# Q's weight quarters issued in another order, Q's last rows on GpSimd's queue, two transposes moved between half passes, K1's copy on ScalarE

## The chip, the core and the metric

The kernel runs on one NeuronCore of a Trainium2 chip. The metric is the device time of one execution in microseconds (us); lower is better. All moments below are counted from the start of the profiled span.

## The reference

Input x has 2048 tokens of 576 numbers (bf16). It is normalized without scale or shift, and two blocks read the result xn; their outputs and x itself are added:

```python
xn = _layernorm(x, axis=-1)
return x + _A_ref(xn, A_wqkv, A_wo) + _B_ref(xn, B_w_gate, B_w_up, B_w_down)
```

Block A is linear attention with 32 heads of 18: q, k, v = xn @ wqkv; phi(t) = (t + 1 if t > 0 else exp(t)) + 1e-6 is applied to q and k; kv and z are sums over all tokens, the head output is (phi(q) kv) / (phi(q) z + 1e-6), and wo follows. Block B is (gelu(xn @ w_gate) * (xn @ w_up)) @ w_down with 4608 hidden columns. The two blocks share nothing but xn.

## The kernel before

**Tiling.** The 2048 tokens are 16 tiles of 128 tokens ("tile n"; 0 to 15). A contraction over the 576 columns takes four chunks of 128 rows (`kt` 0 to 3) and one of 64 (`kt` 4, "the ends"). `_Unit` (L239 to L281) computes a product as two half passes: TensorE is used as two row groups of 64 (LO and HI), which write two banks of PSUM (the matmul accumulators) at the same time. In the first half pass, `rows`, LO writes the left half of the output and HI the right one; in the second, `p2`, they swap. Between the two, the row groups have to take turns on a bank: `swap` puts a semaphore wait on GpSimd's queue (POOL) that TensorE's second half pass waits for. It is called the unit's *turn*.

**The head.** What the change touches is the first 17 us or so. There the kernel loads x tile by tile, computes statistics and norms, brings xn into the transposed layout `xnT` (or, for tiles 0 and 1, the centred copy `xcT`), and starts the products K0, K1, Q0, Q1 and so on (`_Token`: K or Q of one tile) as soon as inputs are there. The gate-and-up units g0, g1 and so on (`_Raw`) come next, and from there the rest of the kernel follows.

For tile n below 4 the chain is: load of x; `stats` in two halves and `aggr` (VectorE, DVE); `rstd` (ScalarE, ACT); `norm` (DVE); `transposes` (TensorE, L359 to L362; called t0 to t3 below) into two PSUM banks; `tp_copy` (L364 to L367), which copies one bank to `xnT` on ScalarE and the other on VectorE. Tile 1 has its mean and square sum from ScalarE. Tiles 0 and 1 are transposed before their rstd is known; rstd is multiplied in when their product is copied out by `raw` (K0 and Q0 on ScalarE, K1 and Q1 on VectorE).

**Loads.** `x` of tiles 0 to 3 are single loads of 144 KB. K's columns of wqkv (rows 0 to 511) are one load of 576 KB. Q's are four quarters of 144 KB: rows LO or HI of each chunk, left or right half of the columns. Named here by rows and half, Q's first half pass reads LO-0 and HI-1, its second LO-1 and HI-0. The rows 512 to 575 of K and of Q, the ends, are two small loads each (`load_w_ends`), read at the end of a second half pass. `wr` holds the ends of gate and up (`load_ends`). Loads are issued on SP's queue unless another is named, and in the order of the program. The framework hands eight completion semaphores in turn to the loads issued by SP and by ScalarE, and the ninth load waits until the first holder has landed. So, before, LO-1 waits for the load of K's columns, and HI-0 for x of tile 1.

**Order of the work.** The head's steps are listed as `step(...)` with an engine, an assumed duration, a rank and what they come after. `in_order` (L77 to L94) plays them through once with those assumed times and writes the instructions in the order found, so a changed assumption (`X_AT`, `DMA_FREE`, a `ready`) can reorder an engine's queue, which the hardware then executes strictly in that order. TensorE's order alone is fixed by hand in `line`: a name is the first half pass of a unit, "t2" the transposes of tile 2. In the kernel before, a second half pass follows as soon as two units are open; "." forces one.

Before, the queues are:

- TensorE: t0, t1, K0 first, K1 first, K0 second, Q0 first, K1 second, t2, Q1 first, Q0 second, K2 first, Q1 second, Q2 first, K2 second, t3, Q2 second, K3 first, Q3 first, K3 second, g0 first, and so on.
- VectorE around tiles 2 and 3: stats and aggr 2, norms 1 and 2, raw K1, its half of the copy of t2, stats and aggr 3, norm 3, raw Q1, its half of the copy of t3, then phi of K2 and Q2.
- POOL: K's ends (2 loads), the copies `twin` that pad x, tile 1's mean, the ends of gate and up (2 loads), twin 2, turns K0, K1 and Q0, the load of x for tiles 4 and 5, turn Q1, twin 3 (which waits for x of tile 3), turn K2 and so on.
- SP: x0, K's columns, x2, LO-0, HI-1, x3, LO-1, HI-0, the DMA transpose of tile 0 (`xnU` 0), wg and wu of block 0, wg of block 1, the DMA transpose of tile 1, x of tiles 6 and 7, and so on. x1 and Q's ends are issued by ScalarE.

Of the kernel before, what the change touches and what calls it, by code (L numbers as in the profile page):

```python
# [25 lines left out]
TPC = SC // P  # L26
HALF = D // 2
# [12 lines left out]
RAW = 14  # L40
# [7 lines left out]
CENTRED = (0, 1)  # L48
# [40 lines left out]
def kernel(  # L89
# [29 lines left out]

    SYNC = mybir.DependencyInfo(mybir.DependencyClass.Sync, mybir.DependencyReason.DATA)  # L120
    LO, HI = slice(0, HP), slice(HP, P)
    banks, head_banks = _Ring([6, 7, 2, 3, 4, 5, 0, 1]), _Ring([4, 5, 6, 7, 2, 3, 4, 5, 6, 7, 2, 3, 4, 5, 0, 1])

    def two_banks(ring=banks):
        return [ring.next(), ring.next()]
# [43 lines left out]
    def load_w_quarters(which, halves):  # L169

        for rows, half in zip((LO, HI), halves):
            c = which * D + half * HALF
            view = A_wqkv[0:4 * P, c:c + HALF].rearrange("(kt p) c -> p kt c", p=P)
            nc.sync.dma_start(wqkv_sb[rows, 0:4, c:c + HALF], view[rows])  # L174
# [9 lines left out]

    gu_blocks, wr_pairs = {}, {}

    def load_ends(i, on=nc.sync):
        c = slice(GUB * P * (i % NB), GUB * P * (i % NB + 2))
        wr = wr_pairs[i // 2] = wr_bufs.next()
        on.dma_start(wr[LO, :], B_w_gate[512:576, c])  # L190
        on.dma_start(wr[HI, :], B_w_up[512:576, c])

    def load_gu(i, part):

# [187 lines left out]

    for n in range(4, NS, 2):
        on, sp, at = ("POOL", 0.75, 9.2) if n == 4 else ("SP", 0.58, 6.0)
        load(("x", n), sp, 295, 9.0 if n == 4 else 7.0 + 2.5 * (n - 10), [("turn", "Q0")] * (n == 4), lambda n=n: load_x(n, 2, nc.gpsimd if n == 4 else nc.sync), ready=at, on=on)
    step("ends", "POOL", 1.4, 3.0, [("mean", 1)], lambda: load_ends(0, nc.gpsimd))

    for n in range(NS):
        first = 1.5 * n if n < 4 else 9.0 + 3.0 * (n - 4)
        both = n // 2 * 2  # L390
        after_x = [("x", both)] if n >= 4 else []
        x_at = X_AT[n] if n < 4 else 12.6 if n < 8 else 2.1 * both + 3.0
        if n < 4:
            step(("twin", n), "POOL", 0.2, first, [], lambda n=n: x_twin(n, 1), ready=10.1 if n == 3 else x_at)
        elif n == both:
            step(("twin", n), "POOL", 0.25, first, after_x, lambda n=n: x_twin(n, 2), ready=max(2.6 * n + 3.0, 14.6))
        twin = ("twin", n if n < 4 else both)
        if n != 1:
            for h in range(2):
                step(("stats", n, h), "DVE", 0.42, first, after_x + [("raw", "K1")] * (n == 3) + [("phi", "Q2")] * (n == 4) + [("phi", "K5")] * (n in (12, 13)), lambda n=n, h=h: ln_half(n, h), ready=x_at)  # L400
            step(("aggr", n), "DVE", 0.2, first, [("stats", n, 0), ("stats", n, 1)], lambda n=n: ln_aggr(n), tail=0.05)
        if n in CENTRED:
            if n:
                step(("sum", n), "ACT", 0.78, first - 3.0, [], lambda n=n: act_sum(n), ready=x_at)
                step(("mean", n), "POOL", 0.54, first - 3.0, [("sum", n)], lambda n=n: act_mean(n), tail=-0.27)
                step(("aggr", n), "ACT", 0.95, first + 2.0, [("mean", n), ("xnT", 1, 0)], lambda n=n: act_square(n))
            mean = ("mean", n) if n else ("aggr", n)
            step(("centre", n), "DVE", 0.45, first - 0.5, [mean, twin], lambda n=n: centre(n), tail=0.05)
        if n not in (1, 2) and n < 6:
            step(("rstd", n), "ACT", 0.5, first - 2.0 * (n == 3), [("aggr", n)], lambda n=n: ln_rstd(n, 1))  # L410
        elif n == both:
            m = min(n, 1) if n < 6 else n
            step(("rstd", n), "ACT", 0.46, first, [("aggr", m), ("aggr", m + 1)], lambda m=m: ln_rstd(m, 2))
            if n == 2:
                steps[("rstd", 1)] = _Step("none", 0.0, first, [("rstd", 2)], lambda: None, 0.0, 0.0)
        ready = [("rstd", n if n < 6 else both), twin]
        if NORM[n] == "A":
            step(("bias", n), "POOL", 0.27, first, ready[:1], lambda n=n: ln_bias(n))
            ready.append(("bias", n))
        on, took = ("ACT", 0.92) if NORM[n] == "A" else ("DVE", 0.45)  # L420
        if n < HEAD:
            late = n in CENTRED
            step(("norm", n), on, took, 2.5 if late else first, ready + [("tp", n)] * late, lambda n=n: ln_norm(n), tail=0.05)
            step(("tp", n), "PE", 0.2, 0, [("centre" if late else "norm", n)], lambda n=n: transposes(n), tail=0.15)
            for i, copied in enumerate((0.44, 0.30)):
                step(("xnT", n, i), "DVE" if i else "ACT", copied, first - 1.0, [("tp", n)], lambda n=n, i=i: tp_copy(n, i), tail=0.02)
            steps[("xnT", n)] = _Step("none", 0.0, first, [("xnT", n, 0), ("xnT", n, 1)], lambda: None, 0.0, 0.0)
            if late:
                load(("xnU", n), 1.25, 80, first + 2, [("norm", n)], lambda n=n: dma_transposes(n))
        else:  # L430
            step(("norm", n), on, took, first, ready, lambda n=n: ln_norm(n), tail=0.05)
            load(("xnT", n), 1.25, 80, first + 2, [("norm", n)], lambda n=n: dma_transposes(n))

    class _Token:
# [14 lines left out]

        def raw(self):  # L450
            dst = (pk if self.kind == "K" else pq)[:, self.n, :].rearrange("p (h c) -> p h c", h=2)
            if self.n == 0:
                nc.scalar.activation(out=dst, in_=self.acc, func=ACT.Identity, scale=rstd[:, 0:1])
            elif self.n == 1:
                nc.vector.tensor_scalar(out=dst, in0=self.acc, scalar1=rstd[:, self.n:self.n + 1], scalar2=None, op0=ALU.mult)
            else:
                nc.scalar.copy(out=dst, in_=self.acc)
            self.acc = dst
# [28 lines left out]
                out=hT[:, self.f:self.f + NF + 1:NF, :], in_=ps_all[:, self.two[0]:self.two[0] + 2, :],  # L487
            )

    line = ["t0", "t1", "K0", "K1", "Q0", "t2", "Q1", "K2", "Q2", "t3", ".", "K3", "Q3"] + [f"g{i}" for i in range(LEAD)]  # L490
    for i in range(12):
        line += [f"K{i + 4}"] + ([f"g{i + LEAD}"] if i + LEAD < RAW else [])

    owner, pending = {}, []

# [23 lines left out]
    def p2_step(u):  # L519
        n = int(u.name[1:])  # L520
        pe(("p2", u.name), u.t2, [("turn", u.name)], u.unit_p2)
        if u.name[0] in "KQ":
            later = u.name in RAW_T
            if later:
                step(("raw", u.name), *(("DVE", 0.76) if n == 1 else ("ACT", 0.9 if n == 0 else 0.66)), u.at, [("p2", u.name), ("rstd", n)] + [("norm", 3)] * (u.name == "Q1"), u.body.raw)
# [11 lines left out]
    for name in line:  # L537
# [2 lines left out]
            continue  # L540
        kind, n = name[0], int(name[1:])
        if kind == "t":
            pe(("tp", n), 0, [], None)
            if name == "t0":
                pe("spin", 0.27, [], lambda: row_spin(5))
            continue
# [11 lines left out]
        else:  # L558
            u.body = _Raw(n)
            b = u.body.two  # L560
            blk = n // GUB
            after = [("xnU" if m in CENTRED else "xnT", m) for m in range(TPC)] + [("gu", blk, i) for i in range(2)] + ["ends"] * (blk == 0)
# [10 lines left out]
        if len(pending) == 2:  # L573
            p2_step(pending.pop(0))
    while pending:
        p2_step(pending.pop(0))

# [7 lines left out]
    for i in range(1, NS):  # L585
# [420 lines left out]
```

## Time and profile before

| what | value |
|---|---|
| median of 3 runs | 509.84 us (509.75 to 509.9) |
| profiled execution, its own time | 509.41 us |
| its span | 507.6 us |
| mean granted TensorE clock | 0.999 |
| TensorE matmul busy (PE) | 501.9 us, 99% of the span |
| TensorE busy from 5 to 10 us, from 10 to 15 us | 4.32 us, 4.04 us |
| TensorE busy from 15 to 60 us | all of it |

The span runs from the first to the last instruction of the profile; 1.8 us of the execution's own time lie around it. In the profile, PE is the matmul part of TensorE and PEld its weight load; SPq, ACTq and POOLq are the queues that issue loads. A wait is named by the instruction that released it. The landing of a load is the moment at which its semaphore is full.

### The profile page before, as it was taken

How to read it: one execution, taken by the hardware profiler on the slowest of the kernel's cores; microseconds unless marked ns; L12 is line 12 of the kernel's file. 1: busy time of each engine (PE TensorE's matmuls, PEld its weight loads, DVE VectorE, ACT ScalarE, POOL GpSimd, SP SyncE). 2: the span in 40 equal slices, each digit the busy share in tenths (PEclk: the TensorE clock that was granted, in tenths of full speed). 3: DMA queues.
4: the chain of work that ended last, by engine and by line, in shares of the span. 5: the costliest groups of instructions: out<-in, count | busy, mean ns of one | idle time of the engine just before them, and what ended most of it. 6: DMA issues, size and time to landing. Idle time of an engine off the chain costs nothing.

```text
span 507.6 us, 11204 instructions
## 1 busy us (share of the span) xinstructions
PE 501.9 (99%) x4765; PEld 305.1 (60%) x4765; DVE 229.7 (45%) x478; ACT 152.8 (30%) x266; POOL 12.6 (2%) x39
## 2 busy tenths in 40 slices
PE   7999999999999999999999999999999999999997
PEld 6666775446777444445777444445877444445774
DVE  5859796774101665553102665553102665543100
ACT  4788734335000432233000432233000432232000
POOL 4111100000000000000000000000000000000000
PEclk9999999999999999999999999999999999999999
DMA  9997956993200555654000455653000455630000
GB/s 214 252 204 175 269 130 185 261 266 107 71 13 26 145 149 160 175 161 108 12 13 27 143 149 160 175 160 109 13 12 28 143 149 158 176 109 14 13 13 23
DMA packets 115131, 61.76 MB, mean 122 GB/s; under 512 B 24642, under 2 KB 114954, under 8 KB 115082
## 3 DMA queue, kind: packets, MB, share of 16 engines
q1 hardware_dynamic: 114570, 60.33, 44.9%
q8 instruction: 37, 0.61, 0.5%
q0 software_dynamic: 208, 0.50, 0.3%
q10 hardware_dynamic: 304, 0.22, 0.1%
q14 instruction: 12, 0.10, 0.1%
HBM read 53.60 MB, written 2.36 MB: 110 GB/s over the span
## 4 chain that ended last, share of the span: by engine, by line
PE 97%; DMA 2%; SPq 0%; issue 0%; DVE 0%
PE ps_all L258 62%; PE ps_all L921 28%; PE ps_all L622 3%; PE ps_all L926 3%; DMA wqkv_sb<-in_A_wqkv_dram 2%; PE ps_all L909 0%; PE ps_all L630 0%; PE ps_all L649 0%; PE ps_all L861 0%; SPq L174 0%; SPq L163 0%; DVE res L935 0%; PE ps_all L668 0%; PE ps_all L362 0%
## 5 line engine op out<-in xcount | busy, mean ns | idle before, releaser
L258 PE MATMUL ps_all<-xnT,wg 64*128 64x512 bf16 x1152 | 273.7, 376 | 0.0
L258 PE MATMUL ps_all<-xnT,wu 64*128 64x512 bf16 x1152 | 273.1, 376 | 0.0
L258 PEld LDWEIGHTS <-wg 64*128 64x128 bf16 x1152 | 108.3, 94 | 66.6
L258 PEld LDWEIGHTS <-wu 64*128 64x128 bf16 x1152 | 108.3, 94 | 65.4
L814 DVE TENSOR_TENSOR hT<-ps_all,gl 128x512 bf16<-128x512 f32 x130 | 89.8, 691 | 104.2 <-ACT gl L813 104.1
L921 PEld LDWEIGHTS <-hT 128*128 128x128 bf16 x1152 | 110.8, 98 | 30.9 <-issue 1.2
L813 ACT ACTIVATE gl<-ps_all 128x512 f32<-128x512 f32 x130 | 77.6, 597 | 164.1 <-PE ps_all L258 163.7
L935 DVE TENSOR_TENSOR res<-ps_all,x_sb 128x288 bf16<-128x288 f32 (+2 forms) x32 | 13.8, 454 | 146.3 <-PE ps_all L926 88.1
L921 PE MATMUL ps_all<-wd_a,hT 128*128 128x288 bf16 (+2 forms) x512 | 68.3, 286 | 0.0
L258 PE MATMUL ps_all<-xnT,wr 64*128 64x512 bf16 x288 | 54.8, 376 | 0.0
L921 PE MATMUL ps_all<-hT 128*128 128x288 bf16 (+2 forms) x384 | 52.4, 286 | 0.0
L835 ACT ACTIVATE gl<-ps_all 128x288 f32<-128x288 f32 x24 | 9.2, 409 | 121.4 <-PE ps_all L258 119.9
L921 PE MATMUL ps_all<-wd_m,hT 128*128 128x288 bf16 (+2 forms) x256 | 36.8, 286 | 0.0
L258 PEld LDWEIGHTS <-xnT 64*128 64x128 bf16 x504 | 27.0, 94 | 6.3 <-ACT xnT L367 0.2
L258 PEld LDWEIGHTS <-wr 64*128 64x128 bf16 x288 | 14.3, 94 | 16.4
L926 PE MATMUL ps_all<-m_sb,pqT 128*128 128x288 bf16 (+2 forms) x128 | 20.9, 286 | 0.0
L258 PE MATMUL ps_all<-wqkv_sb,xnT 64*128 64x288 bf16 x256 | 20.2, 283 | 0.0
L622 PE MATMUL ps_all<-hT,xn 128*128 128x288 bf16 x128 | 16.2, 286 | 0.0
L486 ACT CAST hT<-ps_all 128x1024 bf16<-128x1024 f32 x14 | 14.1, 1007 | 3.9 <-PE ps_all L258 3.7
L622 PEld LDWEIGHTS <-xn 128*128 128x128 bf16 x128 | 12.4, 98 | 3.7 <-issue 0.7
L926 PEld LDWEIGHTS <-pqT 128*128 128x128 bf16 x128 | 12.4, 98 | 3.3
L258 PE MATMUL ps_all<-wo,xnT 64*128 64x288 bf16 x216 | 13.7, 283 | 0.0
(100 smaller groups left out, 248.4 us busy)
## 6 DMA issues: line engine op xcount, KB each, us to landing
wg<-in_B_w_gate_dram SPq DMA_DIRECT2D x72, 256.0 KB, 3.0
wu<-in_B_w_up_dram SPq DMA_DIRECT2D x72, 256.0 KB, 3.5
wd_a<-in_B_w_down_dram SPq DMA_DIRECT2D x4, 576.0 KB, 7.1
wr<-in_B_w_gate_dram SPq DMA_DIRECT2D x35, 64.0 KB, 3.1
wr<-in_B_w_up_dram SPq DMA_DIRECT2D x35, 64.0 KB, 2.8
out_dram<-res SPq DMA_DIRECT2D x15, 144.0 KB, 1.8
hT<-in_B_w_down_dram SPq DMA_DIRECT2D x4, 432.0 KB, 5.8
x_sb<-in_A_x_dram SPq DMA_DIRECT2D x5, 288.0 KB, 4.6
```

The lines of the kernel that those rows point to most:

```text
L258: return nc.tensor.matmul(self.outs[i], lhsT=self.lhs(i, rows, kt), rhs=self.rhs(i, rows, kt), start=start, stop=stop, skip_group_check=True,)
L486: nc.scalar.copy(out=hT[:, self.f:self.f + NF + 1:NF, :], in_=ps_all[:, self.two[0]:self.two[0] + 2, :],)
L622: nc.tensor.matmul(ps_all[:, two[hf], :HALF], lhsT=xn[:, n, kt * P:(kt + 1) * P], rhs=pk[:, n, hf * HALF:(hf + 1) * HALF], start=(n == gra ...
L813: nc.scalar.activation(out=gl[:], in_=ps_all[:, b[0], :], func=ACT.Gelu_apprx_tanh)
L814: nc.vector.tensor_tensor(out=hT[:, GUB * k + i, :], in0=ps_all[:, b[1], :], in1=gl[:], op=ALU.mult)
L835: nc.scalar.activation(out=e[:, :HALF], in_=acc, func=ACT.Exp)
L921: nc.tensor.matmul(self.acc(hf), lhsT=hT[:, f, j * P:(j + 1) * P], rhs=wd(f)[:, self.parts[hf]], start=(f == 0 and not paired), stop=False ...
L926: nc.tensor.matmul(self.acc(hf), lhsT=pqT[:, c, self.ts], rhs=m_sb[:, c, self.parts[hf]], start=False, stop=(paired and c == 3), skip_grou ...
L935: nc.vector.tensor_tensor(out=self.res[:, hs], in0=self.acc(hf), in1=x_sb[:, self.n, hs], op=ALU.add)
```

## The change

Five things change, all in the head.

1. SP's loads are in the order x0, K's columns, LO-0, x2, HI-1, LO-1, HI-0, x3. Q's ends leave ScalarE's queue, so every Q quarter is among the first eight of the framework's loads and waits for no semaphore; x3 is the ninth and waits for x0's.
2. Q's ends are issued by GpSimd after tile 1's mean, in the place where the ends of gate and up were. Those two are issued by GpSimd one by one, after turns K1 and Q0. The load of x for tiles 4 and 5 moves from behind turn Q0 to behind turn K2.
3. In TensorE's order Q1's first half pass is now before t2, and Q1's second before K2's first. With the second half passes written out, the order is: K0 first, K1 first, K0 second, Q0 first, K1 second, Q1 first, t2, Q0 second, Q1 second, K2 first, Q2 first, K2 second, t3, Q2 second, K3 first, Q3 first, K3 second, and on as before. t2 and t3 get other PSUM banks (4 and 5; 2 and 3), and the rings of banks are reordered; t2 now waits for raw K0, t3 for raw Q0.
4. Raw K1 moves from VectorE to ScalarE, behind raw K0 and ahead of ScalarE's copy of t2; raw Q0 comes after that copy.
5. Assumed times change (x2 and x3 later, the first DMA transpose earlier), and tile 3's stats lose their place behind raw K1. In the built program VectorE's queue is now: norms 1 and 2, the first half of stats 3, its half of the copy of t2, the second half of stats 3, aggr 3, norm 3, raw Q1. On POOL the queue is: Q's ends, turn K0, twin 2, turn K1, one wr load, turn Q0, the other, turn Q1, twin 3, turn K2, x of tiles 4 and 5. On SP the DMA transpose of tile 1 comes before wg of block 1.

```diff
-    banks, head_banks = _Ring([6, 7, 2, 3, 4, 5, 0, 1]), _Ring([4, 5, 6, 7, 2, 3, 4, 5, 6, 7, 2, 3, 4, 5, 0, 1])
+    banks, head_banks = _Ring([6, 7, 4, 5, 0, 1, 2, 3]), _Ring([4, 5, 6, 7, 2, 3, 0, 1, 6, 7, 4, 5, 0, 1, 2, 3])
+    tp_banks = (0, 2, 4, 2)
...
     load_w_main(1)
+    load_w_quarter(0, LO, 0)
     load_x(2, 1)
-    load_w_quarters(0, (0, 1))
-    load_w_ends(0, nc.scalar)
+    load_w_quarter(0, HI, 1)
+    load_w_quarter(0, LO, 1)
+    load_w_quarter(0, HI, 0)
     load_x(3, 1)
-    load_w_quarters(0, (1, 0))
...
-        return ps_all[:, b + 2 * (n == 1), :].bitcast(BF16).rearrange("p (k t) -> p k t", t=HP)
+        return ps_all[:, tp_banks[n] + b, :].bitcast(BF16).rearrange("p (k t) -> p k t", t=HP)
...
-    X_AT = [3.40, 3.80, 6.40, 8.60]
+    X_AT = [3.40, 3.80, 6.90, 9.30]
...
-    DMA_FREE = 9.5
+    DMA_FREE = 9.8
...
-        load(("x", n), sp, 295, ..., [("turn", "Q0")] * (n == 4), ...)
-    step("ends", "POOL", 1.4, 3.0, [("mean", 1)], lambda: load_ends(0, nc.gpsimd))
+        load(("x", n), sp, 295, ..., [("turn", "K2")] * (n == 4), ...)
+    step(("ends", "Q"), "POOL", 1.3, 3.0, [("mean", 1)], lambda: load_w_ends(0, nc.gpsimd))
+    for part, turn in enumerate(("K1", "Q0")):
+        step(("ends", part), "POOL", 0.7, 3.0, [("turn", turn)], lambda part=part: load_ends(0, nc.gpsimd, (part,)))
...
-            if self.n == 0:
-                nc.scalar.activation(out=dst, in_=self.acc, func=ACT.Identity, scale=rstd[:, 0:1])
+            if self.n == 0 or (self.n, self.kind) == (1, "K"):
+                nc.scalar.activation(out=dst, in_=self.acc, func=ACT.Identity, scale=rstd[:, self.n:self.n + 1])
...
-    line = ["t0", "t1", "K0", "K1", "Q0", "t2", "Q1", "K2", "Q2", "t3", ".", "K3", "Q3"] + [f"g{i}" for i in range(LEAD)]
+    line = "t0 t1 K0 K1 . Q0 . Q1 t2 . . K2 Q2 . t3 . K3 Q3 .".split()
...
-        ("xnU", 0), ("gu", 0, 0), ("gu", 0, 1), ("gu", 1, 0), ("xnU", 1), ...
+        ("xnU", 0), ("gu", 0, 0), ("gu", 0, 1), ("xnU", 1), ("gu", 1, 0), ...
...
-    steps[(("xnU", 0), "q")].ready = 7.2
+    steps[(("xnU", 0), "q")].ready = 6.3
```

More of the change, by code (lines that the diff above doesn't have):

```diff
@@ L167, in load_w_main, with load_w_quarter @@
         nc.sync.dma_start(wqkv_sb[:, 0:4, c], A_wqkv[0:4 * P, c].rearrange("(kt p) c -> p kt c", p=P))
[L169 to L174, printed above, removed]
+    def load_w_quarter(which, rows, half):
+        c = which * D + half * HALF
+        view = A_wqkv[0:4 * P, c:c + HALF].rearrange("(kt p) c -> p kt c", p=P)
+        nc.sync.dma_start(wqkv_sb[rows, 0:4, c:c + HALF], view[rows])
     def load_w_ends(which, on=nc.sync):
@@ L185, with load_ends @@
     gu_blocks, wr_pairs = {}, {}
-    def load_ends(i, on=nc.sync):
+    def load_ends(i, on=nc.sync, parts=(0, 1)):
         c = slice(GUB * P * (i % NB), GUB * P * (i % NB + 2))
-        wr = wr_pairs[i // 2] = wr_bufs.next()
-        on.dma_start(wr[LO, :], B_w_gate[512:576, c])
-        on.dma_start(wr[HI, :], B_w_up[512:576, c])
+        if parts[0] == 0:
+            wr_pairs[i // 2] = wr_bufs.next()
+        for part in parts:
+            on.dma_start(wr_pairs[i // 2][(LO, HI)[part], :], (B_w_gate, B_w_up)[part][512:576, c])
     def load_gu(i, part):
@@ L384 @@
         on, sp, at = ("POOL", 0.75, 9.2) if n == 4 else ("SP", 0.58, 6.0)
-        load(("x", n), sp, 295, 9.0 if n == 4 else 7.0 + 2.5 * (n - 10), [("turn", "Q0")] * (n == 4), lambda n=n: load_x(n, 2, nc.gpsimd if n == 4 else nc.sync), ready=at, on=on)
-    step("ends", "POOL", 1.4, 3.0, [("mean", 1)], lambda: load_ends(0, nc.gpsimd))
+        load(("x", n), sp, 295, 9.0 if n == 4 else 7.0 + 2.5 * (n - 10), [("turn", "K2")] * (n == 4), lambda n=n: load_x(n, 2, nc.gpsimd if n == 4 else nc.sync), ready=at, on=on)
+    step(("ends", "Q"), "POOL", 1.3, 3.0, [("mean", 1)], lambda: load_w_ends(0, nc.gpsimd))
+    for part, turn in enumerate(("K1", "Q0")):
+        step(("ends", part), "POOL", 0.7, 3.0, [("turn", turn)], lambda part=part: load_ends(0, nc.gpsimd, (part,)))
     for n in range(NS):
@@ L399 @@
             for h in range(2):
-                step(("stats", n, h), "DVE", 0.42, first, after_x + [("raw", "K1")] * (n == 3) + [("phi", "Q2")] * (n == 4) + [("phi", "K5")] * (n in (12, 13)), lambda n=n, h=h: ln_half(n, h), ready=x_at)
+                step(("stats", n, h), "DVE", 0.42, first, after_x + [("phi", "Q2")] * (n in (4, 5)) + [("phi", "K5")] * (n in (12, 13)), lambda n=n, h=h: ln_half(n, h), ready=x_at)
             step(("aggr", n), "DVE", 0.2, first, [("stats", n, 0), ("stats", n, 1)], lambda n=n: ln_aggr(n), tail=0.05)
@@ L488, in out @@
             )
-    line = ["t0", "t1", "K0", "K1", "Q0", "t2", "Q1", "K2", "Q2", "t3", ".", "K3", "Q3"] + [f"g{i}" for i in range(LEAD)]
+    line = "t0 t1 K0 K1 . Q0 . Q1 t2 . . K2 Q2 . t3 . K3 Q3 .".split()
+    follow = [f"g{i}" for i in range(LEAD)]
     for i in range(12):
-        line += [f"K{i + 4}"] + ([f"g{i + LEAD}"] if i + LEAD < RAW else [])
+        follow += [f"K{i + 4}"] + ([f"g{i + LEAD}"] if i + LEAD < RAW else [])
+    for name in follow:
+        line += [name, "."]
     owner, pending = {}, []
@@ L524, in p2_step @@
             if later:
-                step(("raw", u.name), *(("DVE", 0.76) if n == 1 else ("ACT", 0.9 if n == 0 else 0.66)), u.at, [("p2", u.name), ("rstd", n)] + [("norm", 3)] * (u.name == "Q1"), u.body.raw)
+                step(("raw", u.name), *(("DVE", 0.82) if u.name == "Q1" else ("ACT", 0.75 if n < 2 else 0.66)), u.at, [("p2", u.name), ("rstd", n)] + [("norm", 3)] * (u.name == "Q1") + [("xnT", 2, 0)] * (u.name == "Q0"), u.body.raw)
             ready, rank = ((LATER, 60.0) if u.name[0] == "K" else (LATER + 16.0, 70.0)) if later else (0.0, u.at - 3.0 * (u.name == "K4"))
@@ L542 @@
         if kind == "t":
+            two = (tp_banks[n], tp_banks[n] + 1)
+            steps[("tp", n)].after = steps[("tp", n)].after + owner.get(two, [])
             pe(("tp", n), 0, [], None)
+            owner[two] = [("xnT", n, 0), ("xnT", n, 1)]
             if name == "t0":
@@ L561 @@
             blk = n // GUB
-            after = [("xnU" if m in CENTRED else "xnT", m) for m in range(TPC)] + [("gu", blk, i) for i in range(2)] + ["ends"] * (blk == 0)
+            after = [("xnU" if m in CENTRED else "xnT", m) for m in range(TPC)] + [("gu", blk, i) for i in range(2)] + [("ends", 0), ("ends", 1)] * (blk == 0)
             t1, u.t2 = 1.08, 0.865
@@ L572 @@
         pending.append(u)
-        if len(pending) == 2:
-            p2_step(pending.pop(0))
     while pending:
@@ L590 @@
     loads = [
-        ("xnU", 0), ("gu", 0, 0), ("gu", 0, 1), ("gu", 1, 0), ("xnU", 1), ("x", 6), ("gu", 1, 1), ("x", 8), ("gu", 2, 0), ("gu", 2, 1), ("x", 10),
+        ("xnU", 0), ("gu", 0, 0), ("gu", 0, 1), ("xnU", 1), ("gu", 1, 0), ("x", 6), ("gu", 1, 1), ("x", 8), ("gu", 2, 0), ("gu", 2, 1), ("x", 10),
         ("xnT", 4), ("gu", 3, 0), ("xnT", 5), ("gu", 3, 1), ("gu", 4, 0), ("xnT", 6), ("gu", 4, 1), ("x", 12), ("xnT", 7), ("gu", 5, 0),
```

## The prediction

> **What bounds the kernel now.** I read the page first, then the chain of waits over the first 30 us, TensorE's timeline there, and the DMA view in short windows. The page's busy times:
>
> ```profile
> PE 501.9 (99%) x4765; PEld 305.1 (60%) x4765; DVE 229.7 (45%) x478; ACT 152.8 (30%) x266; POOL 12.6 (2%) x39
> ```
>
> TensorE sets the time. From 15 to 60 us it is busy throughout, so a change in the head counts by one thing: when g0 starts (16.71 us). The chain of waits (start, length, what) shows what holds the head:
>
> ```profile
> 1.27 4.72 DMA wqkv_sb<-in_A_wqkv_dram
> 5.99 0.02 issue
> 6.01 0.61 SPq L174
> ...
> 6.66 4.71 DMA wqkv_sb<-in_A_wqkv_dram
> 11.37 0.04 issue
> 11.41 2.90 PE ps_all L258 x45
> ```
>
> K's columns land at 5.99; only then LO-1 is issued, then HI-0, which lands at 11.37. TensorE's timeline shows where it stands still:
>
> ```profile
> 7.51 0.30 PE L258 MATMUL ps_all<-w_ends,xcT 64*128 64x288 bf16 x2
> 7.87 0.28 PE L258 MATMUL ps_all<-wqkv_sb,xcT 64*128 64x288 bf16 x1
> 8.53 1.14 PE L258 MATMUL ps_all<-wqkv_sb,xcT 64*128 64x288 bf16 x15 [0.38 <-DMA wqkv_sb<-in_A_wqkv_dram]
> ...
> 9.53 0.32 PE L362 MATMUL ps_all<-ident,xn 64*128 64x64 bf16 x7
> ...
> 11.41 0.65 PE L258 MATMUL ps_all<-wqkv_sb,xcT 64*128 64x288 bf16 x7 [0.96 <-DMA wqkv_sb<-in_A_wqkv_dram]
> ...
> 14.12 0.32 PE L362 MATMUL ps_all<-ident,xn 64*128 64x64 bf16 x7
> ```
>
> Units follow at 0.49 us for a first half pass (24 matmuls from 6.04 to 7.51 are three) and 0.12 more for a second; t2 and t3 take 0.25 each. From 6.04, eight first and seven second passes and two transposes are 3.92 + 4.27 + 0.50 = 8.7 us; g0 came 10.67 later. The head thus holds about 1.95 us of standing still: 0.9 at 7.64 to 8.53 (for LO-0 and HI-1), 1.1 before 11.41 (HI-0), 0.2 before K3. More than 2 us (0.4%) can't be won.
>
> **Were the loads late because they were issued late?** Mostly not. The DMA view from 8.5 to 10 us, then its upper rows from 9.6 to 11.4 (40 slices each, busy tenths and GB/s):
>
> ```profile
> DMA  9999989989999999999999999999998999998999
> ...
> q8 instruction: 1, 0.02, 5.1%
> ```
>
> ```profile
> DMA  9999989995999911910000000000000109999898
> GB/s 169 208 172 208 213 161 208 183 119 121 110 87 63 75 30 30 11 13 13 13 13 0 26 11 17 17 17 17 17 17 17 23 17 216 279 258 302 250 262 262
> ```
>
> The engines were busy right up to about 10 us: quarters issued at 6.0 stood behind earlier loads, so an earlier issue only changes the order in line. Then nearly all fell idle, and a trickle of some 17 GB/s lasted to 11.1. The q8 row says why: one instruction fetch, 5.1% of 16 engines for 1.5 us, is 1.22 us of one engine. In the trace's records of single packets it is one read of 16,384 bytes at 8.54, just after TensorE passed its wait for HI-1; from its end at 9.76 one chain of 16 packets of 576 bytes (a sixteenth of a quarter, HI-0's) runs to 10.66. HI-0 landed only when this engine was through. LO-1 had landed at 10.01 (6.01 + 4.0), so a quarter's 0.65 later, 10.65, was HI-0's turn; the fetch cost it 0.7 us.
>
> The Trainium skill ("Runtime: NRT & Kernel Launch", section "Instruction fetch mechanics") has instructions refilled in 16 KiB blocks of 256, at a cost that is mostly hidden. The block agrees with the trace (37 fetches, 0.61 MB in q8's row), the hiding doesn't here. By that rule the loads below would keep their turn, which is the rival B.
>
> **Loads after the change.** Steps between landings: HI-1 8.5, then x3 9.0 is 0.55 for an x tile; LO-0 at 7.87 to HI-1 is 0.65 for a quarter. From K's 5.99: LO-0 6.65, x2 7.2 to 7.4 (before 6.79), HI-1 about 8.2, as x2 and two quarters still lie in front, but not Q's ends (72 KB, half a quarter, 0.3). LO-1 follows at 8.85, HI-0 at 9.5 plus 0.3 for Q's ends on GpSimd, and x3 at 10.0 to 10.4. So x3 (before 9.0) pays for the quarters. The fetch is tied to the place in TensorE's program, which up to Q0 is the same; it comes at HI-1's 8.2 and holds one engine to 9.4, with HI-0 and x3 still to move. I add the 0.7 seen on HI-0, up to the fetch's whole 1.22: HI-0 9.8 to 10.5, x3 10.7 (10.6 to 11.4).
>
> **TensorE after the change.** Q0's rest starts at 8.2 instead of 8.53. From there to t2 was 1.0, so K1's second pass ends at 9.2 and Q1's first at 9.7. t2 needs norm 2: x2 to t2 was 6.79 to 9.53, 2.74, so 10.0; it ends at 10.3, when HI-0 is there. Q0's and Q1's second passes end at 11.5. K2 needs VectorE's half of the copy of t2, now queued behind the first half of stats 3, which waits for x3: 10.7 + 0.41 + 0.31 and about 0.2 of signalling, 11.6. K2 and Q2 first and K2 second end at 13.2. t3 needs x3's chain: two halves of stats 0.82, the copy 0.31, aggr 0.24, rstd 0.72 (7.86 to 8.58 for tile 2), norm 0.45, and 0.2 to the first matmul (13.91 to 14.12): 2.7. That is 13.4, later than 13.2. Before, t3 was at 14.12: 0.7 won. At K3 the raw Q1 and the copy still follow norm 3 on VectorE, so its 0.2 stays and g0 keeps its 2.6 behind t3. I take off 0.1 for x3's open end and get 0.6.
>
> **What else moves, at nothing.** Raw K1 on ScalarE is 0.74 (raw Q0's row) instead of 0.82 on VectorE: ScalarE idled 0.83 before its copy of t2 and 1.84 before raw Q0, which hides it (uncovered, 0.74 on that copy). Behind it now wait that copy and raw Q0; raw K0 ends about 9.7, raw K1 10.4, the copy 10.8, before 11.5. Q's ends on POOL: the wr loads issued in the same place took 3.7 and 4.1 us, K's ends 4.9 and 5.0; issued at 5.2 and 5.8 they land at 9.3 to 10.8, needed about 10.8 at the end of Q0's second pass: 0 to 0.1. Turn K0 stands behind these two issues (6.4), K0's second pass is due at 7.0. Turn K1 stands behind twin 2 (7.3 + 0.24), due 8.7; turn Q0 behind a wr issue of 0.6, due 10.3; turn Q1 behind the other; turn K2 behind twin 3, so x3, due 12.5. The wr loads land about 12 to 13.5, for g0 at 16. x of tiles 4 and 5 is issued about 12.1 instead of 9.80; with its 3.9 it lands at 16.0, before stats 4 (17.0). At worst, 6.4 as x of tiles 10 and 11 took, it is 18.5, which moves tile 4's transpose by 1.5; that landed at 23.9, for K4 at 26.17, so 2.2 are free. Tile 1's DMA transpose lands earlier (before 16.0, for g0). New banks cost only if raw K0 ends after norm 2 (9.7 against 9.9).
>
> Putting Q's ends on another queue gives no room by itself. The Trainium skill ("DMA: Bandwidth & Descriptors", section "Issuing engines are not separate DMA queues") says loads of all issuing engines share the same 16 and that another issuer saves only issue time; what is won here is 0.3 at HI-1 because they come later, which the sum has from rows.
>
> **Sum.** The profiled execution took 509.41, its span 507.6 with 1.8 around it; less 0.6 is 508.8. The median, 509.84, is 0.43 above that execution; less 0.6 is 509.2.
>
> **Rivals.** A, the forecast: the fetch delays x3 and t3 waits for norm 3; g0 0.1 to 0.9 earlier, 509.7 to 508.9. For it: the fetch sits right behind the wait for HI-1. Chance 0.44.
>
> B: the fetch misses x3 (its engine is ahead, or it comes elsewhere), which lands at 10.0 to 10.2. t3 then waits for TensorE's own order: t2 at 10.0, K2 at 11.5, t3 at 13.1; 1.0 won, up to 1.4 if x2 lands at 6.9 and nothing waits at t2: 508.4 to 508.8. For it: by 8.54 that engine had finished LO-1's share, so it ran ahead. Chance 0.42.
>
> C, slower: x3, now last in line with VectorE and twin 3 stopped at it, lands later than 11.42. From there t3, at x3 + 2.7, is later than 14.12, one for one; from 12.45 it costs over 1.0 us: 511. Against it: that is 7.5 us after issue at about 4.95, and the longest in the head was 5.4 (HI-1), anywhere near 6.4. For it: two more quarters, a fetch and a wr load go before it. Chance 0.14, most of it beyond 12.45 if other orders on VectorE slip with it.
>
> D, that the freed semaphores do nothing, since the engines were busy: the order in line still brings HI-0 ahead of x3, so this is A's lower end.
>
> **Numbers.** About 0.2% (1.0 us) is what a measurement of this kernel can tell from no change. A gives 0.42 within and 0.02 faster; B, astride the border, 0.36 faster and 0.06 within; C 0.10 slower and 0.04 within. Faster 0.38, same 0.52, slower 0.10. The range of 508.4 to 510.0 leaves out C's upper part and B's lowest; A's own is 508.9 to 509.7.
>
> **What would show it.** Right: LO-1 and HI-0 issued by 5 us; no wait of TensorE near 11.4; HI-1's wait to about 8.2; x3 landing at 10.6 or later with VectorE's stats 3 waiting for it; t3 near 13.4, g0 near 16.1; TensorE busy from 15 to 60. Wrong: x3 by 10.2 and g0 before 15.8 (B); t3 after 14.12 (C); or a new stall at K4, t2, or behind a turn.

## The result, and the profile after

| what | before | after |
|---|---|---|
| median | 509.86 us (7 runs, 509.75 to 510.31) | 511.37 us (7 runs, 510.02 to 511.99) |
| ratio after to before, 95% interval | | 1.0026 (1.0014 to 1.0038) |
| profiled execution, its span | 509.41, 507.6 | 511.37, 509.5 |
| mean granted TensorE clock | 0.999 | 1.0 |

The change costs about 1.5 us; the forecast was 0.6 us won. The runs after are also spread over 2 us, those before over 0.6. All ratios in this document leave out the one run, of the variant e13 below, that took 585.2 us at a granted clock of 0.851. TensorE's busy time on the page is the same, 502.3 us for 501.9:

```profile
PE 502.3 (99%) x4765; PEld 301.8 (59%) x4765; DVE 229.2 (45%) x477; ACT 153.2 (30%) x267; POOL 13.6 (3%) x41
```

So the loss is standing still. TensorE's timeline of after (start, length, what; in brackets the idle time ahead and what ended it) has it in three places:

```profile
7.96 1.14 PE L259 MATMUL ps_all<-wqkv_sb,xcT 64*128 64x288 bf16 x15 [0.18 <-DMA wqkv_sb<-in_A_wqkv_dram]
...
9.70 0.32 PE L363 MATMUL ps_all<-ident,xn 64*128 64x64 bf16 x10
9.84 0.67 PE L259 MATMUL ps_all<-wqkv_sb,xcT 64*128 64x288 bf16 x8
11.84 0.30 PE L259 MATMUL ps_all<-w_ends,xcT 64*128 64x288 bf16 x2 [1.33 <-DMA w_ends<-in_A_wqkv_dram]
...
14.17 0.33 PE L363 MATMUL ps_all<-ident,xn 64*128 64x64 bf16 x10
...
19.96 0.39 PE L259 MATMUL ps_all<-xnT,wu 64*128 64x512 bf16 x1 [0.34 <-POOLq L270]
...
33.98 0.66 PE L259 MATMUL ps_all<-wqkv_sb,xnT 64*128 64x288 bf16 x8 [0.95 <-DMA xnT<-xn]
```

Up to 10.4 the head is ahead of what was forecast: HI-1 is waited for until 7.96 only, t2 comes at 9.70, and Q0's second half pass begins at 9.84, where HI-0 was waited for until 11.41 before. Then its last two matmuls need the ends of Q's weights, and all that was won is gone: t3 at 14.17 (before 14.12), g0 at 16.68 (before 16.71). At 19.96 TensorE waits for a turn on GpSimd's queue (L270), about 0.5 with what the idle figure leaves out (the matmuls before it begin at 19.25, 0.2 apart). At 33.98 it waits for the transposed x of tile 6: K6 could have started near 32.85, behind the last matmuls of K5 at 32.73. K6 begins 17.30 behind g0, where it was 15.55.

The chain of waits says what stands behind these:

```profile
5.27 0.59 POOL w_ends L178
5.87 0.01 issue
5.88 5.92 DMA w_ends<-in_A_wqkv_dram
11.80 0.04 issue
11.84 1.42 PE ps_all L259 x20
...
13.87 5.99 DMA x_sb<-in_A_x_dram
19.86 0.02 issue
19.88 0.83 DVE stats L310 x2
...
27.17 1.10 ACT hT L489 x2
28.27 5.66 DMA xnT<-xn
33.94 0.05 issue
```

Q's ends, issued at 5.88, land at 11.80. The load of x for tiles 4 and 5, moved behind turn K2, is issued at 13.87 (before 9.80) and lands at 19.86 (before 13.7). Twin 4 stops GpSimd's queue until then, with the turn of a gate-and-up unit behind it: the stall at 19.96. Stats 4 follow at 19.88 (before 17.66), and all behind them is about 2.1 later, to tile 6's transpose, which is issued at 28.27 (before 26.18) and takes 5.66 (before 4.8).

The DMA view from 9.6 to 11.9 (40 slices) shows why Q's ends are late:

```profile
DMA  8999999990000000000101010000000101942999
...
q8 instruction: 1, 0.02, 2.8%
```

The view counts a packet in the slice in which it starts: from about 10.1 to 11.5 almost none does. An instruction fetch of 16,384 bytes begins at 9.66 and holds one engine for 1.02; in the trace's completion records 15 of the 16 parts of Q's second end are in by about 10.1, the last at 11.80. The records of single packets show more. From 10.67 to 11.53 packets run one after the other, as on a single engine that catches up. Meanwhile the other engines are not idle but held: 20 packets of a gate or up load (512 bytes each), begun at 10.05 to 10.09, stay open and end together at 11.54 to 11.60. Such a stretch is called a stand below. The kernel before has one too, where the prediction read idle engines: 20 packets of 256 bytes, of tile 0's DMA transpose, stay open until 11.09 to 11.13.

### The profile page after: what moved, and what is told of

It reads as the page before. It is cut to its first block, busy times and chain, and to the rows that moved or that the text cites. A ratio compares the mean times of both kernels' runs of the same rounds, so it can differ in the third digit from the quotient of the medians.

```text
span 509.5 us, 11211 instructions
## 1 busy us (share of the span) xinstructions
PE 502.3 (99%) x4765; PEld 301.8 (59%) x4765; DVE 229.2 (45%) x477; ACT 153.2 (30%) x267; POOL 13.6 (3%) x41
## 4 chain that ended last, share of the span: by engine, by line
PE 93%; DMA 4%; ACT 1%; DVE 0%; issue 0%; POOL 0%; POOLq 0%
PE ps_all L259 58%; PE ps_all L928 28%; PE ps_all L629 3%; PE ps_all L933 3%; DMA x_sb<-in_A_x_dram 2%; DMA w_ends<-in_A_wqkv_dram 1%; DMA xnT<-xn 1%; ACT hT L489 1%; ACT xn L344 0%; PE ps_all L916 0%; PE ps_all L637 0%; DVE stats L310 0%; PE ps_all L656 0%; PE ps_all L868 0%; ACT z_bf L313 0%
## 5 line engine op out<-in xcount | busy, mean ns | idle before, releaser
L259 PEld LDWEIGHTS <-xnT 64*128 64x128 bf16 x504 | 25.1, 94 | 9.1 <-DMA xnT<-xn 1.3
L259 PE MATMUL ps_all<-wqkv_sb,xnT 64*128 64x288 bf16 x256 | 19.6, 283 | 1.0 <-DMA xnT<-xn 1.0
L310 DVE BATCH_NORM_STATS2 stats<-x_sb 128x6 f32<-128x288 bf16 x30 | 12.0, 435 | 6.2 <-DMA x_sb<-in_A_x_dram 6.2
```

Source lines behind the costliest of these rows:

```text
L259: return nc.tensor.matmul(self.outs[i], lhsT=self.lhs(i, rows, kt), rhs=self.rhs(i, rows, kt), start=start, stop=stop, skip_group_check=True,)
L310: nc.vector.bn_stats(out=ln_raw[n][:, h, :], in_=x_sb[:, n, h * HALF:(h + 1) * HALF])
```

## The experiments

Medians are given beside the 509.9 to 510.1 of the kernel before in the same session (for e16 and e17 one run of it, 510.29). This table holds what the profiles show: when g0 began, when x of tiles 4 and 5 landed, when tile 6's transpose was issued and how long it took, and when K6 began. Behind K6 nothing waits: but for the kernel marked *, the span is K6's start + 475.3 to 475.5 in every profile.

| kernel | median us | Q's ends waited for | g0 | x4 landed | tile 6's transpose | K6 | span |
|---|---|---|---|---|---|---|---|
| before | 509.9 | 0 | 16.71 | 13.7 | 26.18 + 4.8 | 32.26 | 507.6 |
| after | 511.37 | 1.33 | 16.68 | 19.9 | 28.27 + 5.7 | 33.98 | 509.5 |
| after, again (e5) | 510.19 | 0 | 15.59 | 18.8 | 27.21 + 5.6 | 32.81 | 508.3 |
| after, third (e17) | 510.55 | 0 | 15.32 | 18.4 | 26.82 + 6.3 | 33.17 | 508.6 |
| e1, x4 early | 509.49 | 0 | 15.84 | 15.1 | 25.88 + 5.9 | 31.84 | 507.3 |
| e2, ends early | 510.88 | 0 | 16.11 | 18.3 | 26.71 + 5.8 | 32.61 | 508.0 |
| e3, both | 509.29 | 0 | 16.39 | 15.1 | 25.92 + 4.9 | 31.95 | 507.3 |
| e4, before with x4 late | 511.10 | 0 | 17.40 | 19.6 | 27.97 + 6.0 | 34.07 | 509.4 |
| e6, after, transpose up* | 509.68 | 0 | 15.43 | 18.4 | 25.02 | 31.50 | 507.4 |
| e14, after, fetch moved | 508.61 | 0 | 15.88 | 17.0 | 26.15 + 4.4 | 31.43 | 506.9 |
| the same, again (e16) | 508.80 | 0 | 15.80 | 18.1 | 26.51 + 4.4 | 31.35 | 506.8 |

The e5, e16 and e17 rows have one time each.

**Which part costs.** Theory: the late x of tiles 4 and 5 (x4), and the ends of Q's weights on GpSimd, each lose time. Rival: it is the new order of SyncE's loads. e1 puts the x load back:

```diff
-... [("turn", "K2")] * (n == 4), lambda n=n: load_x(n, 2, nc.gpsimd if n == 4 else nc.sync) ...
+... [("turn", "Q0")] * (n == 4), lambda n=n: load_x(n, 2, nc.gpsimd if n == 4 else nc.sync) ...
```

> The changed kernel, with one thing put back: GpSimd issues the load of x tiles 4 and 5 behind the turn of Q0, not of K2. No other engine's instructions change. Theory (the late load costs the time): issued near 9.9 instead of 13.87, it lands near 14 to 15 instead of 19.86; the stall of TensorE at 19.96 (0.39) goes, tile 6's transposed x is in before K6 wants it (the stall of 0.95 at 33.0 to 34.0 goes); Q's ends are not touched, so the head still waits near 11.84 and g0 stays near 16.7. The span falls by 1.6 to 1.9, to about 509.6 to 509.9, level with the kernel before (ratio 0.999 to 1.001). Rival (the later stalls come from the new order of loads on SyncE's queue or from tile 1's transpose, not from this load): the stalls stay, time within 0.3 of the changed kernel, about 511.2.

Measured: 509.49, ratio 0.9989 (0.9980 to 0.9998). e2 puts Q's ends back on ScalarE:

```diff
-    step(("ends", "Q"), "POOL", 1.3, 3.0, [("mean", 1)], lambda: load_w_ends(0, nc.gpsimd))
...
-    load_w_quarter(0, LO, 1)
+    load_w_ends(0, nc.scalar); load_w_quarter(0, LO, 1)
```

> The changed kernel, with the ends of Q's weights issued by ScalarE at the start, as before, not by GpSimd at 5.27; nothing else moves. Theory (the two loads on GpSimd in this place lose the head's gain): no wait for the ends at the end of Q0's second pass; TensorE goes on at 10.5 instead of 11.84, t3 comes near 13.0 instead of 14.17 and g0 near 15.5 instead of 16.68. Q's quarters and x3 land 0.2 to 0.4 later, as the 72 KB go in front of them. The load of x tiles 4 and 5 follows the turn of K2, so it also comes about 1.1 earlier and the later stalls stay about as they are: time about 1.1 under the changed kernel, 510.2 (509.9 to 510.6). Rival (the wait is only moved: with the ends in time, x3 or HI-0 is what the head waits for, as the forecast had it): t3 at 13.4 or later, gain 0.7 or less.

Measured: 510.88, ratio 1.0017 (1.0008 to 1.0026). No wait for the ends, but t3 came at 13.48 only: x3 landed late, and stats 3 waited 0.49 for it, to 11.03. That is the rival's path, and the forecast's case A. e3 has both edits:

> Both at once: the changed kernel with the ends of Q's weights on ScalarE at the start, as before, and the load of x tiles 4 and 5 behind the turn of Q0. Theory: the two costs add, so g0 comes near 15.5 and there is no stall behind it: 1.0 to 1.3 under the kernel before, about 508.6 to 508.9 (ratio 0.997 to 0.998). Rival (the two loads share engines with each other and with x3: an x load issued at 9.5 takes x3's place in line, or the head's gain is given back at K4 or K6, since these wait for tile 4's chain, which doesn't come earlier): level with the kernel before, 509.5 to 510.

Measured: 509.29, ratio 0.9983 (0.9975 to 0.9992): faster than the kernel before, by less than expected, as t3 again came late (13.76). e4 moves only the x load, in the kernel before:

> The kernel before, with one thing of the change: GpSimd issues the load of x tiles 4 and 5 behind the turn of K2, not of Q0. Theory: issued near 13 instead of 9.80, it lands near 18 to 20 instead of 13.7; twin 4 and behind it a turn of GpSimd hold TensorE for some 0.3 to 0.5, and tile 6's transpose is late at K6 by about 1: slower by 1.2 to 1.9, about 511.0 to 511.7. Rival (the changed kernel's late stalls belong to its new loads' order): within 0.3 of the kernel before.

Measured: 511.10, ratio 1.0015 (1.0006 to 1.0024). So less the kernel before: after +1.5, x early -0.5, ends early +0.9, both -0.7. The x load is worth 1.6 to 2.0 in the changed kernel and 1.1 in the kernel before. The ends' place comes out at 0.2 to 0.6, but the intervals of after and e2 overlap, and those of e1 and e3, so a gain there is not shown. Of the 1.8 that e4's profiled span is longer, 0.7 is another thing, HI-0 landing at 12.1, not 11.4; the rest is at K6:

```profile
34.07 0.66 PE L258 MATMUL ps_all<-wqkv_sb,xnT 64*128 64x288 bf16 x8 [0.94 <-DMA xnT<-xn]
```

**Are the ends always late?** The changed kernel, unchanged, twice more:

> The changed kernel as it is, profiled once more. Theory L (chance): the ends of Q's weights land in time or late as the instruction fetch of 16 KB happens to stand in front of the one part that is still missing; so the wait for them at the end of Q0's second pass can be anything from 0 to 1.4, and g0 anything from 15.6 to 16.7. Theory F (fixed): issued at 5.27 by GpSimd they always land near 11.8, and the wait of about 1.3 comes again. Under both x of tiles 4 and 5 lands 5 to 6 after its issue behind the turn of K2, and K6 waits for tile 6's transposed x again.

> The changed kernel as it is, profiled a third time. The ends of Q's weights are late by 0 or by 1.2 to 1.4 (510.2 or 511.4 in all); x of tiles 4 and 5 is issued 2.4 or more behind tile 1's transpose, so behind three loads of SyncE, and lands 5.5 to 6 later; K6 waits 0.8 to 1.

Measured: 510.19 and 510.55, no wait for the ends in either, g0 at 15.59 and 15.32. With the late time, 511.37, this is the chance that theory L names: late in one profile of three. What stays in both is x4 (landing 6.0 and 5.9 after its issue) and K6, of e17:

```profile
18.50 0.39 PE L259 MATMUL ps_all<-xnT,wu 64*128 64x512 bf16 x1 [0.23 <-POOLq L270]
...
33.17 0.66 PE L259 MATMUL ps_all<-wqkv_sb,xnT 64*128 64x288 bf16 x8 [1.59 <-DMA xnT<-xn]
```

g0 1.4 earlier than before, and K6 0.9 later.

**Does K6 cap it?** One move in SyncE's list, in after (e6), in e1 (e7) and in e3 (e8):

```diff
-        ... ("xnT", 5), ("gu", 3, 1), ("gu", 4, 0), ("xnT", 6), ("gu", 4, 1), ...
+        ... ("xnT", 5), ("gu", 3, 1), ("xnT", 6), ("gu", 4, 0), ("gu", 4, 1), ...
```

> The changed kernel with one move on SyncE's queue: the DMA transpose of tile 6 goes ahead of the three weight loads (gate and the two remainders) that stood before it; in the changed kernel tile 6 was normalised by about 26.3 and its transpose issued at 28.27. x of tiles 4 and 5 stays late. Theory (the late x costs its time at K6, through tile 6's transpose): issued about 1.9 earlier, it lands near 32.1, K6 waits for nothing (0.95 to 1.3 gone), the stall near 20 stays: time 510.1 to 510.5. Rival (the transpose's 5.7 in flight, or K7 and K8 behind it, make the same wait again): 511 or more.

Measured: 509.68, ratio 0.9993 (0.9983 to 1.0003), runs from 508.76 to 511.32; 1.7 less than after, where about 1 was expected. K6 waits for nothing; some 0.4 comes back in small gaps between 46.7 and 53.

> The same move, on the kernel with the x load of tiles 4 and 5 put back behind the turn of Q0. In that kernel's profile g0 began at 15.84, 0.9 earlier than in the kernel before, but K6 began only 0.4 earlier (31.84 against 32.26), after 0.27 of waiting for tile 6's transpose. Theory (K6 caps what the head can win): with the cap off, K6 comes 15.5 behind g0, at 31.4; median about 509.1, 0.3 to 0.5 under that kernel's 509.49 and 0.8 under the kernel before. Rival (no cap; the profiled wait was chance): 509.4 to 509.6, as without the move.

Measured: 509.60, ratio 0.9988 (0.9979 to 0.9996), no better than e1: in its profile the ends were late instead, by 1.42, so g0 came at 17.00 and the cap was never reached (12 of the 16 parts of the second end were in by 10.35, the other four came from 11.93 on):

```profile
12.16 0.30 PE L259 MATMUL ps_all<-w_ends,xcT 64*128 64x288 bf16 x2 [1.42 <-DMA w_ends<-in_A_wqkv_dram]
```

> The same move, on the kernel with both repairs (ends on ScalarE at the start, x of tiles 4 and 5 behind the turn of Q0). There g0 began at 16.39 and no wait at K6 was seen. Theory (the move is worth only what K6 waits): no difference, 509.2 to 509.4. Rival (an earlier transpose helps further down too, or the three loads now later cost something): more than 0.2 off in either direction.

Measured: 509.29, ratio 0.9982 (0.9974 to 0.9991), the same as e3: the move is worth only what K6 waits.

**Where to put Q's ends, and raw K1.** Both on the kernel of e7. In e9 SyncE issues the ends between HI-0 and x3:

> The kernel with the late x repaired and tile 6's transpose moved up, and with the ends of Q's weights issued by SyncE between HI-0 and x3, not by GpSimd. Theory (the ends are late only as they are queued last, where one held engine is left over): now x3 and the wr loads are last; the ends land with HI-0 near 9.5 to 10.0, x3 0.3 later than in that kernel (10.0 to 10.3) and g0 at 15.5 to 16.0 in nearly every run: median 508.8 to 509.1 and its runs within 0.6 of each other, where that kernel's eleven lay between 508.60 and 509.98. Rival (whatever comes last is late, so now x3): a fetch of 1.0 to 1.3 on one engine holds x3, t3 comes at x3 + 2.7, and the runs are spread as before, median 509.4 or more.

Measured: 509.25, ratio 0.9987 (0.9978 to 0.9996), runs from 508.86 to 509.66. The rival: now both of the last loads are late, the ends waited for 0.49 until 11.40, x3 until about 11.6 (twin 3 at 11.63), g0 at 16.69. In e12 VectorE copies raw K1 again:

> The kernel with the late x repaired and tile 6's transpose moved up, with raw K1 back on VectorE, where it now stands between tile 3's aggregate and its norm. Theory (raw K1's move to ScalarE counts for nothing, as forecast): its 0.82 lies in the 0.72 that norm 3 waits for rstd, so t3 comes 0 to 0.1 later, and ScalarE's copy of t2 0.7 earlier: within 0.2 of the kernel it is compared with (509.4 to 509.8). Rival (VectorE's chain to norm 3 sets t3): t3 0.8 later, median 510 or more.

Measured: 509.37, ratio 0.9989 (0.9980 to 0.9997): no difference from e7 that can be told. In its profile, the slowest of its eleven runs, K2 waited 0.58 for that copy, and g0 waited 1.92 for tile 1's transpose, issued at 9.97 beside the early x load. In e1, e10 and e13, with the x load as early, g0 waited 0.36 to 0.49 for that transpose; that the early x load is what delays it is likely, but no run tests it.

**Moving the fetch.** The 36 warming matmuls at the start (their result is read by nothing) are given as fewer and longer ones, or more and shorter ones, so that TensorE's later instructions stand elsewhere in its program. First on e7, as 9 of 512 columns from a wider tile (e10), and as 72 of 64 (e11):

> The kernel with the late x repaired and tile 6's transpose moved up, with TensorE's 36 warming matmuls of 128 columns (a result that nothing reads) given as 9 of 512: the same columns, 54 instructions fewer ahead of the head. Theory (the 16 KB that are read near 10 are TensorE's next instructions, due at a place in its program): the read comes later by the time of 54 instructions, 1.5 to 1.7, near 11.6 instead of 9.9 to 10.2, when the ends of Q's weights are in; these then never wait: median 508.6 to 509.0, the runs within 0.8 of each other. Rival (the read isn't bound to TensorE's place, or isn't what makes the ends late): read near 10 again, runs between 508.6 and 510, median 509.4 to 509.8.

Measured: 509.79, ratio 1.0009 (0.9991 to 1.0027), runs from 509.04 to 514.07. The fetch came at 11.66, as expected, and the ends weren't waited for. But the wider tile's memset (0.27 for 0.11) stands ahead of one on which ScalarE's load of x1 waits; it was issued 0.2 later, the sum of tile 1 began at 4.75, not 3.81 as in e7, and t1 at 6.38. Its time tells nothing of the fetch.

> The other direction: the 36 warming matmuls as 72 of 64 columns, 72 instructions more ahead of the head. Theory: the read comes some 2 earlier, near 8, while Q's quarters and x3 are still moving; the ends of Q's weights are no more late than the rest, and what the read holds now is a quarter (HI-1, LO-1 or HI-0) or x3, by up to 1.2 on one engine of 16; the runs' spread changes its cause, not its size: median 509.0 to 509.8, with no wait for the ends. Rival: read near 10 again and the same as without the change.

Measured: 509.38, ratio 0.9989 (0.9980 to 0.9997). The fetch came at 8.15, as expected, but the ends were waited for (0.37, to 11.71), and x3 was late (t3 14.03). Here more than one engine's parts were kept back: 8 of the 16 parts of x3 came from 10.90 on, and all parts of the ends from 11.04, around the end of a stand of tile 0's transpose (21 packets, until 10.97 to 11.01).

Then with no side effect, nine matmuls that read the same 128 columns four times:

```diff
-            nc.tensor.matmul(ps_all[:, 7, 0:P], lhsT=warm[:], rhs=warm[:], start=True, stop=True)
+            nc.tensor.matmul(ps_all[:, 7, :].rearrange("p (r c) -> p r c", r=4), lhsT=warm[:], rhs=warm[:].unsqueeze(1).to_broadcast([P, 4, P]), start=True, stop=True)
...
-    spin(NWARM)
+    spin(NWARM // 4)
```

> The kernel with the late x repaired and tile 6's transpose moved up, with TensorE's 36 warming matmuls of 128 columns (a result that nothing reads) given as 9 of 512 that read the same 128 columns four times: 54 instructions fewer, and no other engine changed. Theory (the fetch makes the ends of Q's weights late): it comes near 11.6 instead of 10.0, the ends are in by 10.5 in all runs; median 508.6 to 509.1. Rival (the ends are late for another reason): runs spread from 508.6 to 510 as without it, median 509.4 to 509.7.

Measured, on e7: 508.80, ratio 0.9977 (0.9968 to 0.9986). The time is as the theory has it, the fetch is not: it came at 10.13 (10.04 in e7's profile), when the ends were just in.

> The changed kernel with that one edit: only the fetch moves; x of tiles 4 and 5 stays behind the turn of K2. Theory: no wait for the ends, g0 near 15.5, and then the stalls of the late x: K6 near 32.7, as in the profile of the changed kernel with the ends in time (510.19): median 510.0 to 510.4, about 1.1 under the changed kernel's 511.37 and still over the kernel before. Rival: 511.0 to 511.5, no difference.

Measured, on after and with nothing else changed: 508.61, ratio 0.9974 (0.9964 to 0.9984), runs from 508.12 to 509.32. That is 2.8 less than after, where 1.1 was expected. TensorE's waits from 10 to 36 in its profile (who waits for what: us in total, times, longest) are one line:

```profile
PE ps_all L363 <- ACT hT L456: 0.2, 1, 0.2
```

for these in after's:

```profile
PE ps_all L259 <- DMA w_ends<-in_A_wqkv_dram: 1.3, 1, 1.3
PE ps_all L259 <- DMA xnT<-xn: 1.0, 1, 1.0
PE ps_all L259 <- POOLq L270: 0.3, 1, 0.3
```

The one line left is t2 waiting for raw K0, the price of the new banks that the prediction named. K6 is 2.55 earlier: 0.8 at g0, 0.5 at the turn, 0.1 near 28, 1.1 at K6. x4 landed 4.0 after its issue, not 6.0, as SyncE had issued one load behind tile 1's transpose ahead of it, not four. And tile 6's transpose took 4.4: the third fetch now came at 30.24, when 15 of its 16 parts were in (by 29.55; the last at 30.53).

> The changed kernel with TensorE's warming matmuls given as 9 of 512, profiled once more. Theory P (place in line): SyncE issues tile 1's transpose, then a gate load, x of tiles 6 and 7 and an up load; x of tiles 4 and 5 lands 4.0 after its issue when one of these stands ahead of it and 6 when three do. If SyncE is again late with the transpose (10.7, held for 2.1), x lands near 17 and K6 waits for nothing, time about 508.6; if it is not (10.0 to 10.4, held for 1.2), x lands near 18.8, K6 waits about 0.8, time about 510. Rival: x lands early whatever stands ahead of it, since the fetch is away.

Measured: 508.80. Two loads were ahead of x4, it landed 5.1 after its issue, at 18.1, nearly as late as in e17; yet K6 waited for nothing, as the transpose again took 4.4, with 15 parts in by 30.06 and the fetch at 30.33. So x4's place in line was partly chance; the short transpose came both times. The number of loads ahead is not all of theory P either: in e17, too, two landed before x4, which took 5.9.

> The kernel with both repairs and tile 6's transpose moved up (ends of Q's weights on ScalarE at the start), with the fetch moved as well. Without that, g0 came at 16.4 to 16.7 and x3 at 11.0 to 11.3, in every profile; 509.29. Theory (the fetch, at 8.9 to 9.0, is what holds x3): x3 lands at 10.0 to 10.4, t3 at 12.8 to 13.2, g0 at 15.4 to 15.9: median 508.4 to 508.9, and the runs close together. Rival (x3 is late as it is last behind 72 KB more): x3 10.6 or later, median 509.1 to 509.4.

Measured, on e8: 508.62, ratio 0.9975 (0.9966 to 0.9985), for 509.29: t3 at 13.07, g0 at 15.60. The fetch came at 9.81, where it came at 9.02 and 8.90 in e3 and e8, and x3 landed at 10.00, where it landed at 11.28 and 11.56: here time and moment both fit the theory. In e3 and e8 x3's late parts came within 0.3 of the end of a stand of tile 0's transpose (at 11.02 to 11.05 and 11.28 to 11.33).

## Why the prediction was wrong

**What held.** HI-1 was forecast for about 8.2 and came at 7.96; HI-0 was not waited for; x3's statistics began at 9.83, which is case B and better than the forecast's own A; t3 without the ends' wait came at 13.08 and 12.81 (e5, e17), for 13.1 in B. The head gain is there when the ends are in time (e5, e17): g0 15.3 to 15.6, 1.1 to 1.4 earlier. But it is B's gain. A's own path, on which the forecast of 0.6 stood (the fetch delays x3, and t3 waits for norm 3), did not happen in after, e5 or e17, whose fetch came at 9.66 to 10.19, with x3 in or nearly in. No cost of raw K1's move can be told (e12). The three stalls that the prediction lists in the head, 0.9, 1.1 and 0.2, add up to 2.2, not to its 1.95; its forecast does not use the difference.

**The first step that failed** is the one behind "a change in the head counts by one thing: when g0 starts". It does not: x of tiles 4 and 5 is loaded in the head as well, and K6 hangs on it. In the kernel before, tile 6's transpose was issued at 26.18 and landed at 30.94, and K6 began at 32.26, right behind K5:

```profile
26.18 1.21 SPq L370 DMA_TRANSPOSE xnT<-xn  x1
...
32.14 0.30 PE L258 MATMUL ps_all<-w_ends,xnT 64*128 64x288 bf16 x2
32.26 0.67 PE L258 MATMUL ps_all<-wqkv_sb,xnT 64*128 64x288 bf16 x8
```

This slack of 1.3 was not seen, since no wait showed there. A g0 1.4 earlier uses it up by itself; the late x takes more.

**The second** is the term "x of tiles 4 and 5 ... lands at 16.0 ... At worst ... 18.5 ... 2.2 are free". It was mis-sized and weighed in one place only. The issue was forecast for 12.1 and came at 12.5 to 13.9; in flight it was 5.9 to 6.0, not 3.9, and two (e17), three (e5) or four (after) loads of 256 to 288 KB that SyncE had issued landed before it. The slack was read at K4; the chain of DMA and ScalarE work behind it goes on to K6, and twin 4 has a turn behind it on GpSimd. The prediction named stalls "at K4, t2, or behind a turn" as what would make it wrong, and the turn was one of them; it gave that no price. It is worth 1.6 to 2.0 (after to e1, e2 to e3), more than the whole loss of 1.5, in which the gain at the head is counted.

**The third** is "Q's ends on POOL ... 0 to 0.1". They cost 1.33 in the profiled run, 0 in two others. What the held engine kept back was the last load in line; the prediction put the fetch on HI-0 and x3, because before it had hit HI-0, and did not ask what else was still moving. It also read the held engines as idle, and so counted the harm on the fetch's own engine alone. "The fetch is tied to the place in TensorE's program" was too firm in time: HI-1's wait ended at 7.96 and the fetch came at 9.66; with before's order of TensorE it came at 8.54 and, in e4, at 9.65.

**What most likely joins them** is the fetch. With the late x, tile 6's transpose is needed as soon as it lands, and in six profiles without the edit of the warming matmuls (after, e1, e2, e4, e5, e17) it took 5.6 to 6.3, with a fetch of 0.9 to 1.9 starting 1.2 to 2.6 behind its issue; with that edit and the same place in SyncE's list it took 4.4, twice. The packet records bear this out: in each of the six, 20 or 21 packets of a DMA transpose, most of them begun during the fetch or just ahead of it, stay open and end together 0.8 (e17: 1.5) behind the fetch, and 15 of the 16 parts of tile 6's transpose land 0.8 behind that (in after: fetch 30.54 to 31.47, the packets to 32.27 to 32.30, 15 parts by 33.08, the last at 33.94). In e14 and e16 the 15 parts were in before the fetch began. The change left no slack at two places that a held engine can hit. That the edit is worth some 2.7 is measured (0.9974 against 1.0026); that the fetch is all of it is argued. The rule weighed in the prediction, from the Trainium skill's "Runtime: NRT & Kernel Launch", section "Instruction fetch mechanics", that crossing a block is mostly hidden, does not hold in this head: the last part of the ends came 1.7 behind the other 15.

**Open.** Why the fetch brought no such stand before the parts were in, in the kernel before and in e3: it began in the transpose's flight there too (28.65, 28.84), but 15 parts were in by 29.35 and 29.34, and only the last came late (30.94, 30.86), so 4.8 and 4.9 sufficed. Why e13 is faster with a first fetch that came no later than in e7, by one profile of each; the third came later (31.03), but its transpose stood earlier. Whether SyncE's lateness in e14 belongs to the edit. What a DMA transpose moved out of a fetch's way would win: no run tried it.

The version to keep is e14's or e15's, about 1.3 under the kernel before (0.9974 and 0.9975).

## What to carry to other kernels

A load that is moved later has to be followed to every consumer, not to the first one: write down, for each unit that it feeds in turn, when its input lands and when it is needed, also where the profile shows no wait, since slack shows nowhere. On an in-order queue, what is moved behind a wait brings its wait to everything behind it. When a profile shows one held DMA engine, ask which load will be last in line after the change, and measure several profiles: one run can show it hit or missed.

## What was not expected of the hardware

- An instruction fetch of 16,384 bytes holds one DMA engine for 0.88 to 1.89, and a load that has a part there landed up to 1.7 later. This fits what the Trainium skill says in "DMA: Bandwidth & Descriptors", section "Why a DMA increments its semaphore by 16 and not by 1": engines finish independently and the semaphore counts them. Fifteen parts of Q's second end were in by 10.1, the last at 11.80.
- Behind a fetch the other engines can be held as well. In the stands, some 20 packets, mostly of a DMA transpose, stayed open for up to 2.5 and ended together, while packets ran one after the other as on one engine: until 11.09 to 11.13 in the kernel before, 32.27 to 32.30 in after. By these records a fetch on one engine can make a whole load or transpose late, not only one of its 16 parts.
- The fetches moved with the instructions ahead of them, but not evenly: with 54 fewer the first came at 9.8 to 11.7 (in the changed kernel and its variants without that edit, 8.2 to 10.2), the third at 30.2 to 32.1 (28.1 to 30.5), the second hardly (18.8 to 19.9, for 18.8 to 20.2 in all but one). With 72 more (e11) they came at 8.15, 18.6 and 25.1.
- x4, issued by GpSimd, came behind the loads that SyncE had issued: in after, its 64 packets of 4,608 bytes began to move at 17.9, 4.0 after the issue, and from 14.5 to 17.5 only SyncE's did. With one load ahead, in e14, it was 2.25. The Trainium skill ("DMA: Bandwidth & Descriptors", section "Queues, rings and completion order") has each engine take turns between the queues that it has work for, packet by packet. Once x4's packets had begun they did take turns (43 of SyncE's packets of 1,024 bytes moved among them from 17.9 to 18.8); the four loads ahead moved whole before them. Whether x4 stood ready by then, no run shows.
